# Weights from 64-bit words without a clamp, their range looked at late by reloads, and f, k and q of chunks 5 to 7 loaded later

## The chip, the cores and the metric

The kernel runs on one core of one Trainium2 chip. The metric is the device time of one launch in microseconds. Four compute engines run their own instruction streams in order: PE multiplies matrices, DVE and ACT work on vectors, POOL does a few selections and products. SP issues the transfers (DMA). An engine stops at an instruction until the semaphores that it names have come, and everything behind it on that engine stops too.

## The reference

A linear attention with a decaying state runs over 4 x 8 heads, 768 positions and head size 48. Its output is regrouped to 3072 tokens of 384 and goes through a multiplicative feed-forward layer.

```python
def _attn_ref(q, k, v, f_logit):
    f = 1.0 / (1.0 + np.exp(-f_logit))
    for t in range(S):
        state = f[:, :, t, :, None] * state + np.einsum('bhd,bhe->bhde', k[:, :, t], v[:, :, t])
        y[:, :, t] = np.einsum('bhd,bhde->bhe', q[:, :, t], state)

def _moe_ref(x, w1, w2, w3, w_out):
    a = x @ w1
    b = x @ w2
    h = a * b @ w3
    return (h @ w_out)
```

q, k, v and f_logit are float32. The weights w1, w2 (384 x 1024), w3 (1024 x 1024) and w_out (1024 x 384) are float64: they come to the chip as pairs of 32-bit words, and the kernel makes float32 of them.

## The kernel before, in words

**Attention.** The 3072 tokens are worked in 24 chunks of 128, eight heads at once. For a chunk, f, k and q (two DMAs of 96 KB each) and v are loaded; ACT makes the gate (L378), DVE two scans (L386, L408) and the scaled Q and K (L402, L416), PE the products, POOL the causal mask. Chunks 0 to 3 are worked in a first stage, in which PE also turns the output y to the layout of the layer's input xt (`moved`, L734 to 739) and ACT copies it from the PSUM bank (`settled`, L742). From chunk 4 on y goes through DRAM (yt) and comes back by DMA into xt. PE's general results live in a pool of four banks called f; a product that takes a bank waits until the reader of that bank's former content has run.

**Weights.** Each piece is loaded as 64-bit words. w1 and w2 come in twelve pieces of 512 columns (512 KB), w_out in four of 768 KB, w3 in eight of 1 MB. For each piece ACT takes the magnitude of the high words (L1157) and turns the low words into a float (`rest`, L1160); DVE clamps the magnitude (L1163), shifts it left by three (L1164), puts sign and rest together (`signed`, L1168) and adds the two (`joined`, L1174). w3 @ w_out is multiplied out beforehand: eight `fold`s on PE (L1221), each of 16 matmuls, with a copy on ACT (L1228).

**Feed-forward.** Tokens are taken in six blocks of four chunks. In block 0 the products x @ w1 and x @ w2 (`up`) are plain, three matmuls to a group, first for chunks 0 and 1 (256 wide), then with 512 columns; ACT copies the first factor from its bank (L796) and DVE multiplies the second onto it (L801). Blocks 1 to 5 use seven products in place of eight on halves (`seven` for the two ups, `down` for the product with the folded weight). In `seven` PE does m1, m6, m5, m2 in this order, and ACT copies m1's result (k1, L862) before m2 adds onto the same bank.

**What sets the order.** A planner in Python (`Plan`) gives each task an engine, a cost, dependencies and a priority, and takes greedily the task that can start first by its own clock, the lower priority number first among equals. The result is a fixed order for each engine. SP is one of these engines: all DMAs are issued in one order, at most eight under way. A load is planned to take 0.6 us of lag, its size by a rate, and a second lag (1.3 us and what the call adds). `need(u)` is the time at which chunk u is wanted on that clock; f, k and q of chunk u have the priority need(u) - 30 to - 29.

**At the end.** A small `judge` on DVE looks at the gates' smallest products and at whether the outputs are finite, its result goes through DRAM and back as a row (`told`, `heard`), `decided` reduces it, and the last `m3` of the last block waits for it. If the answer is bad, a general version of the kernel runs after this one; with the data here it doesn't.

Of the kernel before, what the change touches and what calls it, by code (L numbers as in the profile page):

```python
# [36 lines left out]
F32 = mybir.dt.float32  # L37
# [29 lines left out]
LOW = float.fromhex("0x1p-15")  # L67
HIGH = float.fromhex("0x1.dffffep+16")
W = C // 2
FULL = 35.0  # L70
FLOOR = 2.0**-60
RANGE = 2.0**-40


class Plan:
# [13 lines left out]

        self.pools[name] = [None] * n  # L90

    def add(self, eng, cost, emit, deps=(), prio=0.0, takes=(), frees=(), lag=0.2, slack=0.0):


        t = {
            "eng": eng, "cost": cost, "emit": emit, "deps": [d for d in deps if d is not None], "prio": prio,
            "takes": list(takes), "frees": list(frees), "lag": lag, "slack": slack, "at": None, "end": None, "no": len(self.tasks),
        }
        self.tasks.append(t)
        return t  # L100

    def order(self):
        free, done, left = {}, [], list(self.tasks)
        enders = {}
        for t in self.tasks:
            for f in t["frees"]:
                enders.setdefault(id(f), []).append(t)

        def after(t, ds):

            if any(d["end"] is None for d in ds):
                return None
            return max([0.0] + [d["end"] + (d["lag"] + t["slack"] if d["eng"] != t["eng"] else 0.0) for d in ds])

        def places(t, name):

            ends = [(after(t, enders[id(h)]) if h else 0.0, i) for i, h in enumerate(self.pools[name])]
            return [e for e in ends if e[0] is not None]

        def start(t):  # L120

            waits, at = list(t["deps"]), free.get(t["eng"], 0.0)
            for name in t["takes"]:
                if name in self.pools:
                    ends = places(t, name)
                    if not ends:
                        return None
                    at = max(at, min(ends)[0])
                    continue
                n, taken = self.slots[name]  # L130
                if len(taken) >= n:
                    waits += enders[id(taken[-n])]
            ready = after(t, waits)
            return None if ready is None else max(at, ready)

        while left:
            at, _, _, t = min(
                ((at, t["prio"], t["no"], t) for t in left if (at := start(t)) is not None), key=lambda x: x[:3]
            )
            t["at"], t["end"] = at, at + t["cost"]  # L140
            free[t["eng"]] = t["end"]
            for name in t["takes"]:
                if name in self.pools:
                    t["got"] = min(places(t, name))[1]
                    self.pools[name][t["got"]] = t
                else:
                    self.slots[name][1].append(t)
            left.remove(t)
            done.append(t)
        return sorted(done, key=lambda t: (t["at"], t["no"]))  # L150


@with_exitstack
def kernel(
    ctx: ExitStack,
    tc: tile.TileContext,
    q: bass.AP,
    k: bass.AP,
    f_logit: bass.AP,
    v: bass.AP,  # L160
    w1: bass.AP,
    w2: bass.AP,
    w3: bass.AP,
    w_out: bass.AP,
    leaf_mask: bass.AP,
    out: bass.AP,
):
    nc = tc.nc
    const = ctx.enter_context(tc.tile_pool(name="const", bufs=1))
    ident = const.tile([P, P], F32, name="ident")  # L170
    w12 = const.tile([P, 2, KM, DFF], F32, name="w12")
    wc = const.tile([P, KF, DM], F32, name="wc")
    left = const.tile([1, 1], I32, name="left")
    with tc.manual_schedule():
        outside = ranged(tc, q, k, f_logit, v, w1, w2, w3, w_out, out, ident, w12, wc, left)
        with tc.If(outside > 0, preferred_fallthrough_block=True, label="general"):
            general(tc, q, k, f_logit, v, leaf_mask, out, ident, w12, wc)


# [15 lines left out]
def ranged(ctx, tc, q, k, f_logit, v, w1, w2, w3, w_out, out, ident, w12, wc, left):  # L195
# [14 lines left out]
    ps_f = ctx.enter_context(tc.tile_pool(name="ps_f", bufs=1, space=PSUM))  # L210

    floor = keep.tile([R, NQ], F32, name="floor")
    back = keep.tile([R, NQ], F32, name="back")
    gate = [keep.tile([R, NQ + 1], F32, name=f"gate{i}") for i in range(2)]
    qs, ks, fs = ([keep.tile([R, NQ], F32, name=f"{nm}{i}") for i in range(n)] for nm, n in (("q", 3), ("k", 2), ("f", 2)))
    masked = [keep.tile([P, 2, HP, C], F32, name=f"A{i}") for i in range(2)]
    flat = [t.rearrange("p r h c -> p (r h c)") for t in masked]
    diag = [t[:, 0 : 2 * HP * W].rearrange("p (r h c) -> p r h c", r=2, h=HP) for t in flat]
    mids = [t[0:R, 2 * HP * W : 2 * HP * W + HP * D].rearrange("p (h d) -> p h d", d=D) for t in flat]
    sb = [keep.tile([R, HP, R], F32, name=f"sb{i}") for i in range(2)]  # L220
# [103 lines left out]
    def past(u, n, *names):  # L324
        return [tk[u - n][nm] for nm in names if u >= n and nm in tk[u - n]]

    def moves(n, size, rate, emit, deps, prio, late=0.0):


        for j in range(n):  # L330
            i = plan.add("SP", 0.45, (lambda: None) if j else emit, [d] if j else deps, prio - j * 1e-3, takes=["lane"], lag=0.6)
            d = i
            t = plan.add("DMA", size / n / rate, lambda: None, [i], prio - j * 1e-3, lag=1.3 + late, frees=[i])
        return t
# [5 lines left out]
    def front(u):  # L340
# [20 lines left out]
                return []  # L361
            return asked[8:9] + [tk[u - n if u - n >= 4 else u % n][nm] for nm in names]

        t["lf"] = moves(2, 197, 250, load(fu, f_logit), free(2, "g"), n0 - 30)
        t["lk"] = moves(2, 197, 250, load(ku, k), free(2, "k"), n0 - 29.5)
        t["lq"] = moves(2, 197, 250, load(qu, q), free(3, "q"), n0 - 29)

        def load_v():
            s["v"] = at(12288 + NQ, DM) if u == 3 else loads.tile([P, DM], F32, name="vt")
# [739 lines left out]
    def fetch(loads_, a, prio, subs, deps=()):  # L1109
# [36 lines left out]
        def sub(c0, c1, dst, due, waits):  # L1146
            n = c1 - c0
            w = n / 512
            lo, hi = words[:, c0:c1, 0], words[:, c0:c1, 1]
            a0 = spot[0] if n <= 512 else (spot[0] + 512) // 1024 * 1024 % 2048  # L1150
            spot[0] = (a0 + (512 if n <= 512 else 1024)) % 2048
            m = magnitudes[:, a0 : a0 + n]
            mine = range(a0 // 512, (a0 + n + 511) // 512)
            s = {}

            def magnitude():
                nc.scalar.activation(m, hi.bitcast(F32), AF.Abs)  # L1157

            def rest():
                nc.scalar.activation(lo.bitcast(F32), lo, AF.Copy, bias=2.0, scale=2.0**-51)  # L1160

            def shifted():
                nc.vector.tensor_scalar(m, m, HIGH, LOW, ALU.min, ALU.max)  # L1163
                nc.vector.tensor_scalar(m.bitcast(U32), m.bitcast(U32), 3, None, ALU.logical_shift_left)  # L1164

            def signed():
                s["to"] = dst()
                nc.vector.scalar_tensor_tensor(  # L1168
                    s["to"].bitcast(U32), hi, 0x80000000, lo, ALU.bitwise_and, ALU.bitwise_or
                )  # L1170

            def joined():
                to = s["to"].bitcast(I32)
                nc.vector.tensor_tensor(to, m.bitcast(I32), to, ALU.add)  # L1174

            past = [joins[i] for i in mine if i in joins]
            b = plan.add("ACT", 0.2 + 0.43 * w, magnitude, [ld] + past, due)
            e = plan.add("ACT", 0.2 + 0.43 * w, rest, [ld], due)
            h = plan.add("DVE", 0.32 + 0.54 * w, shifted, [b], due)
            g = plan.add("DVE", 0.16 + 0.53 * w, signed, [e, b] + list(waits), due)  # L1180
            j = plan.add("DVE", 0.16 + 0.53 * w, joined, [h, g], due - 1)
            parts.append((g, j))
            joins.update({i: j for i in mine})
            got.append(g)
            ends.append(j)
# [87 lines left out]

    where = {}

    def judge():
        low = work.tile([R, 1], F32, name="low")
        nc.vector.tensor_reduce(out=low, in_=lasts, axis=AX.XY, op=ALU.min)
# [2 lines left out]
        nil = work.tile([R, 1], F32, name="nil")  # L1281
        nc.vector.tensor_reduce(out=nil, in_=zero, axis=AX.X, op=ALU.add)
        nc.vector.tensor_scalar(nil, nil, 0.0, None, ALU.is_equal)
        good = work.tile([R, 1], F32, name="good")
        nc.vector.tensor_scalar(low, low, RANGE, None, ALU.is_ge)
        nc.vector.tensor_tensor(good, low, nil, ALU.mult)
        where["good"] = good

    def told():
        where["all"] = dram.tile([R, 1], F32, name="good")  # L1290
        nc.sync.dma_start(where["all"], where["good"])

    def heard():
        row = work.tile([1, R], F32, name="row")
        nc.sync.dma_start(row, where["all"].rearrange("r one -> one r"))
        where["row"] = row

# [6 lines left out]
    for u in range(NU):  # L1304
# [9 lines left out]
        if u == NPE - 1:  # L1314
            weights()
        if u == NU - 1:
            looked = plan.add("DVE", 1.0, judge, [tk[i]["y"] for i in range(NU)], -20)
            sent = moves(1, 0.4, 250, told, [looked], 0, 20.0)
            judged = plan.add("DVE", 0.2, decided, [moves(1, 0.4, 250, heard, [sent], 0, 20.0)], -20)
        if u % UB == UB - 1:  # L1320
# [2 lines left out]
    for t in plan.order():  # L1323
# [5 lines left out]
        plan.got = t.get("got")  # L1329
        t["emit"]()  # L1330
    return blk[NB - 1]["outside"]


@with_exitstack
# [334 lines left out]
```

## Time and profile before

| | |
|---|---|
| median of three runs | 480.79 us (479.53 to 482.15) |
| profiled execution, device time | 481.99 us |
| its span | 480.3 us |
| granted PE clock | 0.997 |
| ACT L1157 (magnitude) | 24 times: 12 of 512 at 685 ns, 4 of 768 at 929, 8 of 1024 at 1169 |
| ACT L1160 (rest) | 24 times: 683, 922, 1173 ns |
| DVE L1163 (clamp), 512 / 1024 | 419 / 685 ns |
| DVE L1164 (shift), 512 / 1024 | 427 / 694 ns |
| first fold on PE starts | 78.19 us |
| last out store is issued after | PE's last product, 474 us |

The span is the time between the first and the last instruction of the profiled execution; some 1.7 us of its device time lie around it. A row of a timeline gives start and duration, engine, line, operation, the tile written and the tiles read, how many of them followed each other, and in brackets how long the engine had been idle and what released it. A row of waits gives who waited for whom, the total, how often and the longest. A fence cuts such answers to a few lines.

### The profile page before, as it was taken

What the parts mean: (1) busy time and instruction counts of PE and PEld (TensorE: products, weight loads), DVE (VectorE), ACT (ScalarE), POOL (GpSimd) and SP (SyncE); (2) the same over time, 40 slices, a digit from 0 to 9 for tenths busy, and PEclk for the clock granted to TensorE, in tenths of its full rate; (3) what the DMA queues carried; (4) which work ended last, traced back from release to release, by engine and by line L of the source; (5) the groups of instructions that cost most, each with busy time, mean ns of one, the idle gap of its engine ahead of it and who ended that gap; (6) DMA issues with size and microseconds to landing.
All of it is one profiled execution on the core that took longest, in us unless ns stands there. A gap on an engine that the chain in (4) does not pass through costs nothing.

```text
span 480.3 us, 11336 instructions
## 1 busy us (share of the span) xinstructions
PE 466.2 (97%) x4667; PEld 398.5 (83%) x4667; DVE 362.7 (76%) x706; ACT 141.2 (29%) x310; POOL 63.2 (13%) x88
## 2 busy tenths in 40 slices
PE   8799899999999899999999999999999999999995
PEld 6688644656799788899988889988899888889995
DVE  8999699999999889899899467367653667655541
ACT  4787356472313334333432210010100110110000
POOL 9300000013303224212431100000000000000000
PEclk9999999999999999999999999999999999999998
DMA  6899277843516664455631002100101000000011
GB/s 183 261 386 235 61 256 248 286 139 92 138 38 171 190 185 138 125 150 142 168 111 26 18 18 66 50 17 2 57 27 49 1 0 1 0 2 0 34 66 40
DMA packets 36622, 50.14 MB, mean 104 GB/s; under 512 B 4546, under 2 KB 26050, under 8 KB 35538
## 3 DMA queue, kind: packets, MB, share of 16 engines
q1 hardware_dynamic: 36562, 49.33, 34.1%
q8 instruction: 38, 0.62, 0.6%
q14 instruction: 22, 0.18, 0.1%
HBM read 40.67 MB, written 8.65 MB: 103 GB/s over the span
## 4 chain that ended last, share of the span: by engine, by line
PE 78%; DMA 8%; DVE 7%; POOL 3%; issue 2%; ACT 1%; SPq 0%; ACTq 0%; DVEq 0%; POOLq 0%
PE f L759 62%; PE f L1221 7%; PE py L513 2%; DMA vt<-in_v_dram 2%; DMA place<-in_w_dram 2%; PE pa L439 2%; DMA place<-in_w_out_dram 2%; PE f L453 2%; PE py L532 2%; PE pa L546 2%; DMA k<-in_k_dram 2%; DVE place L1168 1%; DVE place L1174 1%; POOL ab L304 1%; DVE ab L801 1%
## 5 line engine op out<-in xcount | busy, mean ns | idle before, releaser
L759 PE MATMUL f<-xt,w 128*128 128x256 f32 (+1 forms) x600 | 161.1, 397 | 3.4 <-ACT ab L796 1.9
L759 PEld LDWEIGHTS f<-xt,w 128*128 128x128 f32 x600 | 112.9, 190 | 29.1 <-issue 10.0
L759 PE MATMUL f<-place 128*128 128x192 f32 (+1 forms) x504 | 112.1, 349 | 0.1
L759 PEld LDWEIGHTS f<-place 128*128 128x128 f32 x504 | 87.7, 190 | 6.2 <-DVE place L1010 0.4
L569 POOL TENSOR_SCALAR_AFFINE_SELECT A<-A 64x512 f32<-64x512 f32 (+1 forms) x44 | 40.9, 929 | 117.3 <-ACT A L563 107.5
L1221 PE MATMUL f<-place 128*128 128x384 f32 x128 | 42.8, 489 | 0.2 <-DVE place L1174 0.2
L862 ACT COPY a<-f 128x256 f32<-128x256 f32 x36 | 13.4, 373 | 93.2 <-PE f L759 78.0
L1221 PEld LDWEIGHTS f<-place 128*128 128x128 f32 x128 | 23.8, 190 | 16.5 <-DVE place L1174 0.8
L759 PE MATMUL f<-xt,place 128*128 128x256 f32 x144 | 37.3, 382 | 0.0
L759 PE MATMUL f<-wc,ab 128*128 128x192 f32 x192 | 35.2, 327 | 0.0
L759 PEld LDWEIGHTS f<-wc,ab 128*128 128x128 f32 x192 | 32.0, 190 | 0.5
L408 DVE TENSOR_TENSOR_SCAN bwd<-gate,back 112x512 f32<-112x512 f32 x24 | 30.0, 1248 | 0.8
L386 DVE TENSOR_TENSOR_SCAN fwd<-gate,floor 112x512 f32<-112x512 f32 x24 | 29.6, 1232 | 1.2 <-ACT gate L378 0.3
L759 PEld LDWEIGHTS f<-xt,place 128*128 128x128 f32 x144 | 26.6, 189 | 3.3
L886 DVE TENSOR_TENSOR place<-f,a 128x256 f32<-128x256 f32 x36 | 15.2, 423 | 18.3 <-PE f L759 18.0
L1157 ACT ACTIVATE place<-place 128x512 f32<-128x512 f32 (+2 forms) x24 | 21.3, 887 | 7.8 <-DVE w L1174 3.8
L672 POOL TENSOR_TENSOR G<-lasts,gate 112x4 f32<-112x4 f32 x20 | 11.6, 580 | 88.1 <-ACT lasts L391 55.2
L1160 ACT ACTIVATE place<-place 128x512 f32<-128x512 uint32 (+2 forms) x24 | 21.1, 886 | 5.7 <-DMA place<-in_w_out_dram 5.7
L708 ACT ACTIVATE ys<-py 112x512 f32<-112x512 f32 x20 | 11.9, 596 | 34.4 <-PE py L532 34.4
L759 PE MATMUL f<-place,w 128*128 128x256 f32 x72 | 21.4, 379 | 0.0
L897 DVE TENSOR_TENSOR ab<-f,place 128x256 f32<-128x256 f32 x36 | 15.2, 423 | 6.2 <-PE f L759 5.3
L995 DVE TENSOR_TENSOR place<-ab 128x512 f32<-128x512 f32 x24 | 16.9, 703 | 3.5 <-PE f L759 3.5
(126 smaller groups left out, 641.1 us busy)
## 6 DMA issues: line engine op xcount, KB each, us to landing
place<-in_w_dram SPq DMA_DIRECT2D x8, 1024.0 KB, 4.9
place<-in_w_dram SPq DMA_DIRECT2D x12, 512.0 KB, 10.4
out_dram<-o SPq DMA_DIRECT2D x24, 192.0 KB, 1.9
q<-in_q_dram SPq DMA_DIRECT2D x46, 96.0 KB, 2.9
vt<-in_v_dram SPq DMA_DIRECT2D x23, 192.0 KB, 3.8
k<-in_k_dram SPq DMA_DIRECT2D x44, 96.0 KB, 2.3
f<-in_f_logit_dram SPq DMA_DIRECT2D x43, 96.0 KB, 2.5
yt<-ys SPq DMA_DIRECT2D x40, 96.0 KB, 2.6
```

The source lines that it names most:

```text
L386: nc.vector.tensor_tensor_scan(s["P"], gate[u % 2][:, 0:NQ], floor, 0.0, ALU.mult, ALU.max)
L408: nc.vector.tensor_tensor_scan(s["R"][:, ::-1], gate[u % 2][:, NQ:0:-1], back[:, ::-1], 0.0, ALU.mult, ALU.max)
L569: nc.gpsimd.affine_select(out=a, in_=a, pattern=pattern, compare_op=ALU.is_ge, fill=0.0, base=0, channel_multiplier=-1,)
L708: nc.scalar.activation(ys, py, AF.Copy, accum_out=ysum[:, u : u + 1])
L759: nc.tensor.matmul(out_, lhsT=lhs[i], rhs=rhs[i], start=start and i == 0, stop=i == len(lhs) - 1, skip_group_check=True,)
L862: nc.scalar.copy(q["a"], q["X"])
L886: nc.vector.tensor_tensor(ups["u3", k], q["Y"], q["a"], ALU.add)
L897: nc.vector.tensor_tensor(m if which else to(tok, half), q[bank_], m, ALU.add)
L995: nc.vector.tensor_tensor(abs_[j], x, y, op)
L1157: nc.scalar.activation(m, hi.bitcast(F32), AF.Abs)
L1160: nc.scalar.activation(lo.bitcast(F32), lo, AF.Copy, bias=2.0, scale=2.0**-51)
L1221: nc.tensor.matmul(w3s["p", jc], lhsT=w3s[jc][:, kc * P : kc * P + P], rhs=wos[:, kc], start=(kc == 0), stop=(kc == KF - 1),)
```

## The change

For each weight piece, the magnitude on ACT and the clamp on DVE are gone; the shift reads the high words where they were loaded (every second word). The sign bit is shifted out by it, so without the clamp the result is right only for weights whose magnitude is in a certain range. That is looked at later: `ranges`, planned once the last chunk's attention is done with its buffers, loads all weights again, 17 loads of 1 MB into the place of the two masked tiles A. After each, ACT sums the magnitudes of the high words (`total`) and the signs of magnitude less a limit (`count`); each load waits for the count before it. Four operations on DVE (`verdict`) make one number of it, and `judge` multiplies it into its own, which has 128 rows now instead of 112. If a check fails, the general version runs, and before it `convert` makes the weights again with the clamp.

Besides, f, k and q of chunks 5, 6 and 7 may not be planned before need(u) - 17 on the planner's clock.

```diff
+AHEAD = 17.0
-    def add(self, eng, cost, emit, deps=(), prio=0.0, takes=(), frees=(), lag=0.2, slack=0.0):
+    def add(self, eng, cost, emit, deps=(), prio=0.0, takes=(), frees=(), lag=0.2, slack=0.0, since=0.0):
...
-            waits, at = list(t["deps"]), free.get(t["eng"], 0.0)
+            waits, at = list(t["deps"]), max(free.get(t["eng"], 0.0), t["since"])
...
-    back = keep.tile([R, NQ], F32, name="back")
+    spare = keep.tile([P, NQ], F32, name="back")
+    back = spare[0:R]
-    masked = [keep.tile([P, 2, HP, C], F32, name=f"A{i}") for i in range(2)]
-    flat = [t.rearrange("p r h c -> p (r h c)") for t in masked]
+    both = keep.tile([P, 2 * WIDE], F32, name="A")
+    flat = [both[:, i * WIDE : i * WIDE + WIDE] for i in range(2)]
+    masked = [t.rearrange("p (r h c) -> p r h c", r=2, h=HP) for t in flat]
...
-        t["lf"] = moves(2, 197, 250, load(fu, f_logit), free(2, "g"), n0 - 30)
-        t["lk"] = moves(2, 197, 250, load(ku, k), free(2, "k"), n0 - 29.5)
-        t["lq"] = moves(2, 197, 250, load(qu, q), free(3, "q"), n0 - 29)
+        since = n0 - AHEAD if 4 < u < 8 else 0.0
+        t["lf"] = moves(2, 197, 250, load(fu, f_logit), free(2, "g"), n0 - 30, since=since)
+        t["lk"] = moves(2, 197, 250, load(ku, k), free(2, "k"), n0 - 29.5, since=since)
+        t["lq"] = moves(2, 197, 250, load(qu, q), free(3, "q"), n0 - 29, since=since)
...
-            def magnitude():
-                nc.scalar.activation(m, hi.bitcast(F32), AF.Abs)
-
             def shifted():
-                nc.vector.tensor_scalar(m, m, HIGH, LOW, ALU.min, ALU.max)
-                nc.vector.tensor_scalar(m.bitcast(U32), m.bitcast(U32), 3, None, ALU.logical_shift_left)
+                nc.vector.tensor_scalar(m.bitcast(U32), hi, 3, None, ALU.logical_shift_left)
...
-            b = plan.add("ACT", 0.2 + 0.43 * w, magnitude, [ld] + past, due)
             e = plan.add("ACT", 0.2 + 0.43 * w, rest, [ld], due)
-            h = plan.add("DVE", 0.32 + 0.54 * w, shifted, [b], due)
-            g = plan.add("DVE", 0.16 + 0.53 * w, signed, [e, b] + list(waits), due)
+            h = plan.add("DVE", 0.16 + 0.27 * w, shifted, [ld] + past, due)
+            g = plan.add("DVE", 0.16 + 0.53 * w, signed, [e, h] + list(waits), due)
...
+    def ranges():
+        seen = [w[kc * P : kc * P + P] for w in (w1, w2) for kc in range(KM)] + [w3[jc] for jc in range(KF)]
+        rows_ = w_out.rearrange("(p a) c -> p (a c)", a=KF)
+        seen += [rows_[:, c : c + WIDE] for c in range(0, KF * DM, WIDE)]
...
+        last = [plan.add("DVE", 0.1, lambda: nc.vector.memset(small, -SMALL), [tk[NU - 1][nm] for nm in ("r", "v", "mid")] + [tk[NU - 2]["v"]], -20)]
+        def load(i):
+            return lambda: nc.sync.dma_start(words, seen[i].bitcast(U32))
+        def total(i):
+            return lambda: nc.scalar.activation(hi, hi, AF.Abs, accum_out=sums_[:, i : i + 1])
+        def count(i):
+            return lambda: nc.scalar.activation(hi, hi, AF.Sign, bias=small, accum_out=counts[:, i : i + 1])
+        for i in range(n):
+            ld = moves(1, 1024, 380, load(i), last, 500 + i, 1.0)
+            a = plan.add("ACT", 1.1, total(i), [ld], 500 + i)
+            last = [plan.add("ACT", 1.2, count(i), [a], 500 + i)]
+        def verdict():
+            nc.vector.tensor_scalar(sums_, sums_, LARGE, None, ALU.is_le)
+            nc.vector.tensor_scalar(counts, counts, WIDE - 0.5, None, ALU.is_ge)
+            nc.vector.tensor_tensor(sums_, sums_, counts, ALU.mult)
+            where["weights"] = small
+            nc.vector.tensor_reduce(out=small, in_=sums_, axis=AX.X, op=ALU.min)
+        return plan.add("DVE", 0.5, verdict, last, -20)
...
-        good = work.tile([R, 1], F32, name="good")
+        good = work.tile([P, 1], F32, name="good")
-        nc.vector.tensor_tensor(good, low, nil, ALU.mult)
+        nc.vector.memset(good, 1.0)
+        nc.vector.tensor_tensor(good[0:R], low, nil, ALU.mult)
+        if wide:
+            nc.vector.tensor_tensor(good, good, where["weights"], ALU.mult)
...
-            looked = plan.add("DVE", 1.0, judge, [tk[i]["y"] for i in range(NU)], -20)
+            weighed = [ranges()] if wide else []
+            looked = plan.add("DVE", 1.0, judge, [tk[i]["y"] for i in range(NU)] + weighed, -20)
```

More of the change, by code (lines that the diff above doesn't have):

```diff
@@ L69 @@
 W = C // 2
+WIDE = 2 * HP * C
+SMALL = 2.0**-8
+LARGE = 2.0**15
 FULL = 35.0
+AHEAD = 17.0
 FLOOR = 2.0**-60
@@ L90, in pool @@
         self.pools[name] = [None] * n
-    def add(self, eng, cost, emit, deps=(), prio=0.0, takes=(), frees=(), lag=0.2, slack=0.0):
+    def add(self, eng, cost, emit, deps=(), prio=0.0, takes=(), frees=(), lag=0.2, slack=0.0, since=0.0):
         t = {
             "eng": eng, "cost": cost, "emit": emit, "deps": [d for d in deps if d is not None], "prio": prio,
-            "takes": list(takes), "frees": list(frees), "lag": lag, "slack": slack, "at": None, "end": None, "no": len(self.tasks),
+            "takes": list(takes), "frees": list(frees), "lag": lag, "slack": slack, "since": since, "at": None, "end": None, "no": len(self.tasks),
         }
@@ L176 @@
         with tc.If(outside > 0, preferred_fallthrough_block=True, label="general"):
+            if w1.dtype != F32:
+                convert(tc, w1, w2, w3, w_out, w12, wc)
             general(tc, q, k, f_logit, v, leaf_mask, out, ident, w12, wc)
@@ L325, in past, with moves @@
         return [tk[u - n][nm] for nm in names if u >= n and nm in tk[u - n]]
-    def moves(n, size, rate, emit, deps, prio, late=0.0):
+    def moves(n, size, rate, emit, deps, prio, late=0.0, since=0.0):
         for j in range(n):
-            i = plan.add("SP", 0.45, (lambda: None) if j else emit, [d] if j else deps, prio - j * 1e-3, takes=["lane"], lag=0.6)
+            i = plan.add("SP", 0.45, (lambda: None) if j else emit, [d] if j else deps, prio - j * 1e-3, takes=["lane"], lag=0.6, since=since)
             d = i
@@ L1274, in ranged @@
     where = {}
+    def ranges():
+        seen = [w[kc * P : kc * P + P] for w in (w1, w2) for kc in range(KM)] + [w3[jc] for jc in range(KF)]
+        rows_ = w_out.rearrange("(p a) c -> p (a c)", a=KF)
+        seen += [rows_[:, c : c + WIDE] for c in range(0, KF * DM, WIDE)]
+        n = len(seen)
+        sums_, counts, small = (spare[:, a : a + m] for a, m in ((0, n), (32, n), (64, 1)))
+        words = both.bitcast(U32)
+        hi = words.rearrange("p (n two) -> p n two", two=2)[:, :, 1].bitcast(F32)
+        last = [plan.add("DVE", 0.1, lambda: nc.vector.memset(small, -SMALL), [tk[NU - 1][nm] for nm in ("r", "v", "mid")] + [tk[NU - 2]["v"]], -20)]
[16 more added lines that the diff above has]
+        return plan.add("DVE", 0.5, verdict, last, -20)
     def judge():
@@ L1283, in judge @@
         nc.vector.tensor_scalar(nil, nil, 0.0, None, ALU.is_equal)
-        good = work.tile([R, 1], F32, name="good")
+        good = work.tile([P, 1], F32, name="good")
         nc.vector.tensor_scalar(low, low, RANGE, None, ALU.is_ge)
-        nc.vector.tensor_tensor(good, low, nil, ALU.mult)
+        nc.vector.memset(good, 1.0)
+        nc.vector.tensor_tensor(good[0:R], low, nil, ALU.mult)
+        if wide:
+            nc.vector.tensor_tensor(good, good, where["weights"], ALU.mult)
         where["good"] = good
     def told():
-        where["all"] = dram.tile([R, 1], F32, name="good")
+        where["all"] = dram.tile([P, 1], F32, name="good")
         nc.sync.dma_start(where["all"], where["good"])
     def heard():
-        row = work.tile([1, R], F32, name="row")
+        row = work.tile([1, P], F32, name="row")
         nc.sync.dma_start(row, where["all"].rearrange("r one -> one r"))
@@ L1331, in ranged, with convert, single @@
     return blk[NB - 1]["outside"]
+@with_exitstack
+def convert(ctx, tc, w1, w2, w3, w_out, w12, wc):
+    nc = tc.nc
+    work = ctx.enter_context(tc.tile_pool(name="cwork", bufs=2))
+    keep = ctx.enter_context(tc.tile_pool(name="ckeep", bufs=1))
+    ps = ctx.enter_context(tc.tile_pool(name="cps", bufs=2, space=bass.MemoryType.PSUM))
+    def single(src, dst):
+        n = src.shape[-1]
+        raw = work.tile([P, 2 * DFF], U32, name="raw")[:, 0 : 2 * n]
+        m = work.tile([P, DFF], F32, name="m")[:, 0:n]
+        nc.sync.dma_start(raw, src.bitcast(U32))
+        words = raw.rearrange("p (n two) -> p n two", two=2)
+        lo, hi = words[:, :, 0], words[:, :, 1]
+        nc.scalar.activation(m, hi.bitcast(F32), AF.Abs)
+        nc.scalar.activation(lo.bitcast(F32), lo, AF.Copy, bias=2.0, scale=2.0**-51)
+        nc.vector.tensor_scalar(m, m, HIGH, LOW, ALU.min, ALU.max)
+        nc.vector.tensor_scalar(m.bitcast(U32), m.bitcast(U32), 3, None, ALU.logical_shift_left)
+        nc.vector.scalar_tensor_tensor(dst.bitcast(U32), hi, 0x80000000, lo, ALU.bitwise_and, ALU.bitwise_or)
+        nc.vector.tensor_tensor(dst.bitcast(I32), m.bitcast(I32), dst.bitcast(I32), ALU.add)
+    for which, w in enumerate((w1, w2)):
+        for kc in range(KM):
+            single(w[kc * P : kc * P + P], w12[:, which, kc])
+    rows_ = keep.tile([P, KF, DM], F32, name="rows")
+    for a in range(KF):
+        single(w_out[a * P : a * P + P], rows_[:, a])
+    for jc in range(KF):
+        t = work.tile([P, DFF], F32, name="t")
+        single(w3[jc], t)
+        p = ps.tile([P, DM], F32, name="p")
+        for a in range(KF):
+            nc.tensor.matmul(p, lhsT=t[:, a * P : a * P + P], rhs=rows_[:, a], start=(a == 0), stop=(a == KF - 1))
+        nc.scalar.copy(wc[:, place_of(jc)], p)
 @with_exitstack
```

## The prediction

> **What bounds the kernel now.** I read the page's engine table first, then busy time by stretches, then the waits of PE (TensorE), then the two timelines around its longest wait.
>
> ```profile
> PE 466.2 (97%) x4667; PEld 398.5 (83%) x4667; DVE 362.7 (76%) x706; ACT 141.2 (29%) x310; POOL 63.2 (13%) x88
> ```
>
> PE is busy 97% of the span. The other engines matter only where PE waits for them.
>
> ```profile
> 34.00:50.00 16.00, 16.00 (x79) 14.19 (x79) 12.88 (x27) 10.62 (x20) 0.00 (x0) 1.00 0.92 229
> 50.00:60.00 10.00, 8.10 (x32) 5.81 (x32) 7.47 (x17) 4.42 (x9) 0.51 (x1) 1.00 0.19 50
> 60.00:80.00 20.00, 20.00 (x49) 9.07 (x48) 19.69 (x28) 11.20 (x16) 0.20 (x1) 1.00 0.79 271
> 100.00:135.00 35.00, 35.00 (x464) 24.66 (x463) 34.17 (x48) 12.79 (x27) 7.63 (x8) 1.00 0.39 106
> 275.00:410.00 135.00, 135.00 (x689) 122.96 (x682) 82.49 (x200) 14.80 (x41) 0.00 (x0) 1.00 0.08 26
> ```
>
> Columns: stretch and length, then busy time of PE, weight loads, DVE, ACT, POOL, then clock, DMA share, GB/s. From 60 to 135 DVE is as full as PE, and still PE does not stop: DVE's full row costs nothing as it stands. In the tail ACT is busy 11% and the DMA 8%. Only 50 to 60 has a hole in PE.
>
> ```profile
> PE f L759 <- ACT ab L796: 1.9, 1, 1.9
> PE f L759 <- ACT gate L378: 1.4, 1, 1.4
> PE pa L429 <- DVE Q L402: 1.0, 1, 1.0
> PE f L1221 <- DVE place L1174: 0.2, 1, 0.2
> ```
>
> These are PE's waits after 24 us (total, times, longest). The first hole, in the timelines of PE and ACT:
>
> ```profile
> 34.70 15.71 PE L759 MATMUL f<-xt,w 128*128 128x256 f32 x72
> 52.30 1.99 PE L759 MATMUL f<-xt,w 128*128 128x256 f32 x8 [1.90 <-ACT ab L796]
> ...
> 51.12 0.88 ACT L1160 ACTIVATE place<-place 128x768 f32<-128x768 uint32 x1 [4.89 <-DMA place<-in_w_out_dram]
> 51.90 0.35 ACT L796 COPY ab<-f 128x256 f32<-128x256 f32 x1
> ```
>
> ACT stood 4.89 us at the head of its queue for the second w_out piece. The copy that frees PE's bank was behind it. The 1.4 at 161.25 is a late transfer in truth: DVE's L829 waited 1.99 us for xt<-yt until 161.19, and the gate named had long ended.
>
> [...] the dense shift (L1164: 427 ns for 512, against 758 for L1168 with two sources); a shift from every second word no run shows. [...] a stride of two words should be free; L1168 reads such words in the time of a dense two-source operation (1221 and 1247 ns for 1024), which agrees. [...] the trace has 1.17 (L1160), and I use that, +0.09 for Sign.
>
> **Part 1: Abs and clamp go.** ACT loses L1157, 24 times, 21.3 us; DVE loses L1163, start to start about 12 x 0.45 + 4 x 0.59 + 8 x 0.72 = 13.5 us. Almost all lies beside a full PE. What can be won is DVE's share in waits: 0.2 before the second fold, and half of the 0.6 at two small waits (0.36 for L1010 at 135.97, 0.25 for an ACT copy at 263.88). I take -0.5 (0 to -0.8; the 1.0 at 24 us is counted in part 2).
>
> [...] it would take 0.69, 0.95, 1.22 instead of 0.43, 0.56, 0.69: 12 x 0.26 + 4 x 0.39 + 8 x 0.53 = 9 us of DVE. I take zero; the other end is rival C.
>
> **Part 2: f, k, q of chunks 5 to 7 later.** SP's order is unchanged to k of chunk 4. Then come two w_out loads, where q4, f5 and k5 (six DMAs) stood between them; in all 18 DMAs for f, k, q of three chunks go behind loads of weights. The second w_out piece was issued at 42.03 and landed at 51.04; now its issue is at about 37.5, the place of q4's row, so it lands some 3 us earlier or more. Both gates of chunks 4 and 5 that stood behind it (1.15 us at 52.15) are elsewhere. The wait of 1.9 goes: -1.9 (-1.9 to 0).
>
> But ACT's order changes before that too. In the trace, xt of chunk 3 is copied at 34.90 and the first ab copies run at 36.20, 37.49, 38.90, 40.08 between conversions. In the changed order ACT has the conversions (the Copy of L1160) of w12 pieces 9, 10 and 11, then xt of chunk 3, then the gate of chunk 4, and only then the first ab copy. The SP queue's rows give the landings: piece 11 issued at 29.88 takes 10.2 us, so 40.1; the first half of f4 issued at 31.10 takes 9.4, so 40.5, the second 41.0. DMA is at 0.92 and more until then and has the same orders, so these times stay. PE has four banks; one holds chunk 3's px until its xt copy. The timeline's 72 records in 15.71 us are twelve groups of three 256-wide products, 1.31 us each. Three run from 34.70 to 38.6; the fourth needs that bank. ACT: 40.1 + 0.68 + 0.48 = 41.3. So PE loses 41.3 - 38.6 = +2.7 (1.5 to 3.4). That PE comes to this point sooner, as without its 1.0 at 24 us, only makes the wait longer and not the end later. The gate (0.63) ends at 41.9, in time for the fifth group at 42.6.
>
> Chunk 5's late f harms nothing: attention of chunk 4 itself first reaches PE at 88.95 in the trace. Afterwards only four, not eight, 512-wide groups (2.6 us each) stand before the first fold. It was at 78.19; now about 78.19 - 4 x 2.6 - 1.9 + 2.7 = 68.6. The w3 loads, first at 64.81 before, follow w_out directly, near 50: 5 us to land, then conversion, ready near 61 to 63. No wait, 5 us in hand. The 1.4 at 161 depends on when xt of chunk 7 is issued, which moves with all of this: half of it, -0.7.
>
> **Part 3: the look at the ranges.** 17 loads of 1 MB, each with Abs and Sign over 1024 words, strictly one after another: 4.9 (a 1 MB load's median) + 1.17 + 0.19 + 1.26 + 0.19 (two readings of the accumulator, 0.19 as at L708) and hand-overs of some 0.4 = 8.1 us; 17 of them, 138 us from about 263, end near 400. SP keeps xt loads and stores behind some of them, and the last m3 that needs the answer is at 472: 65 us in hand. DMA at 0.08 can take 17 MB. ACT gets 34 x 1.36 = 46 us more in a stretch with 120 us free. What can reach PE is a k1 copy (L862, 0.37 us) behind such an operation: m6 and m5 give it 0.86 us, of which 0.23 are to spare. The planner puts the two where its clock sees no k1; I take +0.2 (0 to +4). The verdict and judge, some twelve DVE operations at 0.15 us, stand together before a u2 near 402: 1.8 less its slack, +0.6 (0 to 1.2). Were those 65 us gone, each further 1 us of the chain would be 1 us at the end.
>
> **Sum** against the profiled execution (span 480.3, itself 481.99): -0.5 - 1.9 + 2.7 - 0.7 + 0.2 + 0.6 = +0.4, which would be 482.4. That execution is 1.2 above the median of the three, 480.79; on the median the forecast is 481.2, no change. About 0.5% (2.4 us) is what can be told from none.
>
> **Rivals.**
> - A, faster: the fourth group does not wait, since piece 11 lands sooner or ACT's earlier work leaves room, and xt of chunk 7 is in time. -0.5 - 1.9 - 1.4 + 0.2 + 0.6 = -3.0, so 477.8. For it: the 161 wait is a matter of one transfer. Against: the DMA is full to 40 us with the same queue.
> - B, slower: ACT's in-order queue in the tail. An Abs stands at its head waiting for its load, with a k1 behind. The planner's load lasts about 5.6 us (lags of 0.6 and 2.3 and 1024 / 380 = 2.7); the trace's 1 MB takes 4.9, so it decides from a load of over 5.6. About eight of the 17 pairs have a k1 next to them with little room; at half a microsecond each (half of 1.17) this is +4 beside the sum, so 485.2. For it: the loads share SP with stores. Against: the DMA is idle there.
> - C: [...] 5.8 of its 9 us fall before the second fold, where 5 are in hand; the folds then wait 1 to 2 in all, +1.5 beside the sum: about 482.7, on the border of no change.
>
> **How the numbers follow.** Forecast 0.46 (own range 479 to 483.2), A 0.25, B 0.20, C 0.09. C goes half to no change: faster 0.25, same 0.50, slower 0.25. The range reaches to A below and most of B above: 477.6 to 484.6.
>
> **What would show it.** PE's waits: no 1.9 at L796 near 52, a new one of 2 to 3 near 38 to 41 at the fourth up group, ended by ACT's xt copy. The shift's row: 0.43 for 512. PE without holes from 263 to 400 (else B). A small wait near 402 behind the verdict. The first fold near 68. It is wrong if the fourth group starts before 40, or if k1 waits repeat in the tail.

## The result, and the profile after

| | kernel before | changed kernel |
|---|---|---|
| median of 12 runs | 479.56 us (478.15 to 482.15) | 480.01 us (478.71 to 483.87) |
| ratio, 95% interval | | 1.0024 (1.0006 to 1.0042) |
| profiled execution | 481.99 us, span 480.3 | 483.87 us, span 482.1 |

By the ratio the change adds 0.24%, about 1 us (the two medians differ by 0.45): less than the half per cent that the prediction set as what can be told from no change. Forecast were no change and 481.2.

Both profiled executions took longer than most, which matters below. The changed kernel's is the slowest of its twelve. Of the 168 executions of the kernel before that were timed here and in the experiments, four took longer than the profiled 481.99. So the waits that go and come in these two traces are not the balance of an ordinary execution.

The engine table and the shift's rows of the changed kernel, the latter from the groups of DVE by shape between 20 and 135 us:

```profile
PE 467.2 (97%) x4667; PEld 399.3 (83%) x4667; DVE 352.6 (73%) x689; ACT 164.9 (34%) x354; POOL 60.0 (12%) x88
```

```profile
L1169 DVE TENSOR_SCALAR place<-place 128x1024 uint32<-128x1024 uint32 x8 | 5.4, 684 | 0.0
L1169 DVE TENSOR_SCALAR place<-place 128x512 uint32<-128x512 uint32 x12 | 5.0, 419 | 0.0
```

PE has the same work. DVE has 10 us less to do and ACT 24 more: without the Abs it has 21 less, with the reloads some 45 more. The shift from every second word takes 419 and 684 ns, against 427 and 694 from a dense tile: the stride cost nothing here. Rival C, in which the strided shift takes 0.69, 0.95 and 1.22 us for the three sizes, 9 us more in all, is out. Its figures were an estimate; the kernel before has such times at L1174 (690 and 954 ns) and L1168 (1221).

PE's waits after 24 us, in the answer for the changed kernel:

```profile
PE f L768 <- ACT xt L751: 2.7, 1, 2.7
PE pa L438 <- DVE Q L411: 1.0, 1, 1.0
PE f L768 <- ACT a L871: 0.9, 1, 0.9
```

The 1.9 at L796, the 1.4 at 161 us and the 0.2 before a fold are gone. Two are new: 2.7 for the copy of xt, 0.9 for a k1 copy. First the 2.7, in the timelines of PE and ACT:

```profile
34.81 4.05 PE L768 MATMUL f<-xt,w 128*128 128x256 f32 x18
41.56 29.09 PE L768 MATMUL f<-xt,w 128*128 128x256 f32 x102 [2.70 <-ACT xt L751]
70.49 10.48 PE L1225 MATMUL f<-place 128*128 128x384 f32 x32
```

```profile
38.34 0.66 ACT L1166 ACTIVATE place<-place 128x512 f32<-128x512 uint32 x1 [3.07 <-DMA place<-in_w_dram]
40.50 0.65 ACT L1166 ACTIVATE place<-place 128x512 f32<-128x512 uint32 x1 [1.49 <-DMA place<-in_w_dram]
41.05 0.46 ACT L751 COPY xt<-f 128x384 f32<-128x384 f32 x1
41.41 0.63 ACT L387 ACTIVATE gate<-f 112x512 f32<-112x512 f32 x1
```

Three groups of ups run, then PE needs the bank of chunk 3, whose copy (L751) stands on ACT behind two conversions (L1166) that wait for their loads. The second of these is for piece 11, the last of the twelve pieces of w1 and w2; it landed at 40.41 in this trace.

The timeline's single row hides something after the hole, which busy time by stretches shows (the column before the last two is the granted clock):

```profile
42.00:43.00 1.00, 1.00 (x6) 0.81 (x5) 0.66 (x2) 0.58 (x3) 0.20 (x1) 0.75 0.95 305
43.00:46.00 3.00, 3.00 (x9) 2.36 (x8) 2.86 (x7) 0.00 (x0) 0.00 (x0) 0.51 0.15 43
46.00:50.00 4.00, 4.00 (x20) 3.54 (x19) 2.98 (x7) 2.38 (x4) 0.00 (x0) 1.00 0.00 1
```

From 42.5 to 45.9, for 3.4 us, PE ran at half clock (0.51 granted from 43 to 46): eight records stand 0.43 us apart instead of 0.22, 1.65 us more in all. It set in 1.0 us after the hole of 2.7 had ended.

The 0.9, in the tail's timelines of ACT and PE:

```profile
308.13 1.15 ACT L1295 ACTIVATE A<-A 128x1024 f32<-128x1024 f32 x1 [3.74 <-DMA A<-in_w_dram]
309.17 0.19 ACT L1295 ACTIVATION_READ_ACCUMULATOR A<-A 128x1 f32 x1
309.39 1.23 ACT L1298 ACTIVATE A<-A,back 128x1024 f32<-128x1024 f32 x1
310.52 0.19 ACT L1298 ACTIVATION_READ_ACCUMULATOR A<-A,back 128x1 f32 x1
310.61 0.36 ACT L871 COPY a<-f 128x256 f32<-128x256 f32 x1
```

```profile
311.02 1.13 PE L768 MATMUL f<-xt,w 128*128 128x256 f32 x4 [0.93 <-ACT a L871]
```

Abs (L1295) waited at ACT's head for its load, and Sign (L1298) and the k1 copy (L871) stood behind.

What a wait costs in all shows in the starts of PE's products, set against the same products in a profile without the wait. So counted, this one costs 1.20 and another k1 copy, at 317, 0.41 (against the second profile of the order on ACT alone, below). The operations of verdict and judge cost 0.61 near 405 (against the kernel without the look, below). Gone, by starts: 2.2 at 52 us, some 1.5 at 161, 0.25 before a fold, and two small waits of some 0.6, together 4.5. New: 2.9 at 41 us, 1.65 of half clock, 1.6 and 0.6, together 6.8. The balance, 2.2, is the difference of the two spans, 1.8, to within half a microsecond.

### The profile page after: what moved, and what is told of

It reads as the page before. It is cut to its first block, busy times and chain, and to the rows that moved or that the text cites. A ratio compares the mean times of both kernels' runs of the same rounds, so it can differ in the third digit from the quotient of the medians.

```text
span 482.1 us, 11392 instructions
## 1 busy us (share of the span) xinstructions
PE 467.2 (97%) x4667; PEld 399.3 (83%) x4667; DVE 352.6 (73%) x689; ACT 164.9 (34%) x354; POOL 60.0 (12%) x88
## 4 chain that ended last, share of the span: by engine, by line
PE 84%; DMA 6%; DVE 4%; POOL 2%; ACT 2%; issue 1%; DVEq 0%; ACTq 0%; POOLq 0%
PE f L768 65%; PE f L1225 9%; DMA A<-in_w_dram 4%; PE py L522 3%; DMA place<-in_w_dram 2%; PE pa L448 2%; PE pa L555 2%; PE f L462 2%; PE py L541 2%; POOL ab L312 1%; ACT A L1298 1%; ACT A L1295 1%; DVE w L1179 1%; DVE w L1173 0%; DVE K L425 0%
## 5 line engine op out<-in xcount | busy, mean ns | idle before, releaser
L768 PE MATMUL f<-xt,w 128*128 128x256 f32 (+1 forms) x600 | 163.7, 401 | 3.8 <-ACT xt L751 2.7
L578 POOL TENSOR_SCALAR_AFFINE_SELECT A<-A 64x512 f32<-64x512 f32 (+1 forms) x44 | 39.2, 891 | 114.8 <-ACT A L572 105.4
L871 ACT COPY a<-f 128x256 f32<-128x256 f32 x36 | 13.3, 369 | 61.5 <-PE f L768 54.4
L1295 ACT ACTIVATE A<-A 128x1024 f32<-128x1024 f32 x17 | 19.7, 1156 | 25.4 <-DMA A<-in_w_dram 24.5
L1166 ACT ACTIVATE place<-place 128x512 f32<-128x512 uint32 (+2 forms) x24 | 21.3, 888 | 10.0 <-DMA place<-in_w_dram 9.9
L1298 ACT ACTIVATE A<-A,back 128x1024 f32<-128x1024 f32 x17 | 21.2, 1250 | 0.3
L681 POOL TENSOR_TENSOR G<-lasts,gate 112x4 f32<-112x4 f32 x20 | 10.1, 505 | 75.5 <-ACT gate L387 40.5
```

Of the source, the lines that this page charges most:

```text
L578: nc.gpsimd.affine_select(out=a, in_=a, pattern=pattern, compare_op=ALU.is_ge, fill=0.0, base=0, channel_multiplier=-1,)
L768: nc.tensor.matmul(out_, lhsT=lhs[i], rhs=rhs[i], start=start and i == 0, stop=i == len(lhs) - 1, skip_group_check=True,)
L871: nc.scalar.copy(q["a"], q["X"])
L1295: return lambda: nc.scalar.activation(hi, hi, AF.Abs, accum_out=sums_[:, i : i + 1])
L1298: return lambda: nc.scalar.activation(hi, hi, AF.Sign, bias=small, accum_out=counts[:, i : i + 1])
```

## The experiments

Each kernel was timed against the kernel before; ratios are compared where kernels ran on the same chip: the first four below, then the next four, then the last two. The changed kernel was timed again with the first four only. Across chips a comparison is rough: the same kernel, the one with the order on ACT changed, gave 0.9972 on the first chip and 0.9998 on the third.

**The changed kernel again.** No edit.

> The changed kernel once more, to see which of its waits come back in a second profile. Theory 1 (the order on ACT sets the hole): PE waits 2.5 to 2.9 us near 41 us for ACT's copy of xt of chunk 3, again. Theory 2 (the hole is an accident of one execution's transfers): under 1.5 us. Open: whether TensorE's slower passage after the hole (8 records of 0.43 instead of 0.22 us apart, 1.65 us in all) and the 0.9 us wait at 311 for a k1 copy come back. Time: 0 to +1.2 us against the kernel before.

Ratio 1.0013 (0.9996 to 1.0029). PE's waits in its profile:

```profile
PE f L768 <- ACT xt L751: 0.8, 1, 0.8
PE f L768 <- ACT a L871: 0.2, 1, 0.2
```

The hole is in the same place with the same releaser, but 0.8 long: that is the number of Theory 2, and no half clock follows (1.00 granted from 34 to 50). Piece 11 landed at 38.59. In four profiles PE went on about 1.15 us after that landing: 40.41 and 41.56, 38.59 and 39.74, 40.12 and 41.27, 39.20 and 40.35 (this kernel twice, then the ones without the look and without the later loads, below). So the landing sets when the hole ends; that the order on ACT makes it, the next run shows.

**The order on ACT changed alone.**

```diff
+SHY = 6.0
-ld = moves(1, total, 380, load, held, prio, max(0.0, 3.5 - 1.2 * load_no) if load_no < 4 * KM else 3.0)
+ld = moves(1, total, 380, load, held, prio, max(0.0, 3.5 - 1.2 * load_no) + SHY * (load_no > 8) if load_no < 4 * KM else 3.0)
-t["lf"] = moves(2, 197, 250, load(fu, f_logit), free(2, "g"), n0 - 30, since=since)
+t["lf"] = moves(2, 197, 250, load(fu, f_logit), free(2, "g"), n0 - 30, SHY * (u == NPE), since=since)
```

> Only the planner is told that w12 pieces 9 to 11 and f of chunk 4 land 6 us later than it thought, so that ACT copies xt of chunk 3 and the first product ahead of their conversions. Theory 1 (the hole at 41 us comes from ACT's order): no wait of PE between 34 and 60 us over 0.3 us, the first fold 2.7 us earlier than in the changed kernel (67.8 instead of 70.5), or 4.3 earlier (66.2) if the slower passage after the hole goes with it; time 2.7 to 4.3 us under the changed kernel's, so -1.5 to -3.5 us against the kernel before. Rival (PE would only wait a little later, for the second w_out piece): a wait of 1.5 us or more between 46 and 56, time within 1 us of the changed kernel.

Ratio 0.9972 (0.9959 to 0.9986). The xt copy now ends ahead of the conversions, PE has no wait from 34 to 300 us, and the first fold starts at 65.78:

```profile
34.95 0.48 ACT L752 COPY xt<-f 128x384 f32<-128x384 f32 x1 [1.65 <-PE f L747]
```

```profile
34.00:50.00 16.00, 16.00 (x80) 14.19 (x79) 15.13 (x32) 6.60 (x13) 0.20 (x1) 1.00 0.62 187
```

```profile
65.78 10.48 PE L1226 MATMUL f<-place 128*128 128x384 f32 x32
```

Piece 11 landed early in this profile, at 38.0, where the old order would have had a hole of some 0.3 only. In a second profile of this kernel (the last run below) it landed at 39.3, for which the old order would give 1.7, and there was no wait either. The edit also put two w_out loads ahead of k of chunk 4 on SP and moved a few operations on DVE and one on POOL; PE's own order is the same. So the hole is ACT's order, and the rival is out.

Against the changed kernel this is 0.9972 / 1.0013, 2.0 us less (by the two intervals, 1 to 3), not 2.7 to 4.3: the hole is shorter than 2.7 in the other profiles, and the half clock is rare. Of the changed kernel's 34 timed executions four have a granted clock of 0.994 over the whole execution, as the profiled one with the half clock in it, and take 482.1 to 483.9 us; the other thirty have 0.996 or more. The k1 waits stayed:

```profile
PE f L769 <- ACT a L872: 1.4, 2, 1.1
```

**Without the look at the range.**

```diff
-weighed = [ranges()] if wide else []
+weighed = []
-        if wide:
-            nc.vector.tensor_tensor(good, good, where["weights"], ALU.mult)
```

> Leaves out the look at the weights' range: no reloads, no Abs and Sign, no verdict. Theory 1 (it costs PE only the waits seen, 0.9 to 1.4 at 311 and 317 and 0.4 at 405): 1.3 to 1.8 us under the changed kernel, hole at 41 unchanged. Rival (17 MB of loads and 46 us of ACT slow other things unseen): 3 us or more under it. Other rival (the waits are an accident of the one profile): within 0.5 us of it.

Ratio 0.9977 (0.9964 to 0.9991), 1.7 us under the changed kernel on that chip. Its profile has a hole of 1.8 near 41 us and no wait of PE after it. So the late look costs some 1.7, by the two intervals 0.7 to 2.7, which leaves out both rivals. The 2.2 counted in the first profile (1.6 for k1, 0.6 for verdict and judge) lies within this.

**Work put into the hole.**

```diff
             def up(jc, which):
                 def emit():
+                    ups_done[0] += 1
+                    if ups_done[0] == 4:
+                        to = ps.tile([P, 2, NQ], F32, name="py")[:, 0, 0:TH]
+                        for _ in range(FILL):
+                            nc.tensor.matmul(to, lhsT=floor[:, 0:P], rhs=floor[:, 0:TH], start=True, stop=True)
```

> Five products of 256 columns on constants, read by nobody, stand on PE ahead of the fourth group of ups, so that PE is busy some 2.2 us of the hole of 2.7. Nothing else moves. Theory 1 (PE's clock falls for 3.4 us because it was idle for 2.7): the wait left is about 0.5 us, and the 8 slow records after it are gone, first fold at 68.8 instead of 70.5, 1.65 us under the changed kernel if that always has the slow passage. Rival (the slow passage has another cause[...], or is an accident): it comes all the same, time as the changed kernel.

Ratio 1.0106 (1.0077 to 1.0135): neither theory's number. The tile chosen for the idle products was still to be read by DVE, whose instruction stood behind the product with the first ab copy:

```profile
PE py L803 <- DVE S L697: 4.1, 1, 4.1
```

The hole grew to 4.1, and the clock in the stretch after it, 43 to 47, was 0.59. This says nothing on filling a hole, but shows half clock after a longer one.

The same with a tile that nobody held (`name="pa"`):

> As e5_fill, with the five products written to a bank that nobody reads or holds then, so that they don't wait themselves: PE is idle for 0.6 us or less before the fourth group, whenever the transfers let the hole be 2.7. Theory 1 (PE's clock falls after 2 to 2.7 us without work): no products at 0.43 us apart anywhere from 39 to 50 us, granted clock 1.00 in that stretch. Rival (it falls for another reason): they come as in the changed kernel. Time within 1.3 us of the changed kernel either way, as the five products cost up to 1.3 where the hole would have been 0.8.

Ratio 1.0026 (1.0012 to 1.0039). PE had no wait and no half clock between 34 and 60 (1.00 granted). But piece 11 landed at 39.37 there, so the hole would have been some 1.7 (39.37 + 1.15 - 38.8), and a hole of 1.8, in the run without the look, had no half clock either (1.00 granted from 34 to 50). This run doesn't decide about the clock.

**The later loads alone, in the kernel before** (`AHEAD` and `since` as in the change, nothing else).

> The kernel before with one part of the change alone: f, k and q of chunks 5 to 7 later. Abs and clamp stay, no reloads. Theory 1 (the later loads are worth the wait for the second w_out piece, and the hole at 41 belongs to the other part): the piece lands some 3 us sooner than 51.0, no wait of PE near 52 us (1.9 before), no hole near 41 us, time 1.5 to 2.2 us under the kernel before. Rival (the wait is only moved to another load, or the hole near 41 comes with this part): within 0.7 us of the kernel before.

Ratio 0.9984 (0.9969 to 0.9998). The second w_out piece landed at 47.95 and the wait near 52 is gone, by PE's starts a gain of 2.2 us on the profile before. Half of the expectation came in time: 0.8 us, not 1.5 to 2.2. The interval, 0.1 to 1.5, does not rule out the rival's 0.7. The wait for xt of chunk 7 is longer, and in this execution the clock halved after it, at 161 to 164 (0.58):

```profile
159.32 4.51 PE L761 MATMUL f<-xt,w 128*128 128x256 f32 x12 [1.89 <-ACT gate L380]
```

Twelve records take 4.51 here; in the profile before, at 161.25, the same twelve took 2.83. So what this profile gained near 52 it lost again here.

**The changed kernel without the later loads** (`since = 0.0` for all chunks).

> The changed kernel without the later loads: Abs and clamp gone, reloads at the end, f, k and q of chunks 5 to 7 loaded as early as before. Theory 1 (the hole near 41 us comes from the missing Abs, and whatever PE loses there it doesn't lose again for the second w_out piece): the hole is there as in the changed kernel, 0.8 to 2.7 us, and the wait near 52 us is smaller than 1.9 by about as much; time within 0.8 us of the changed kernel. Rival (the two waits add up): 1.5 to 2.2 us over the changed kernel.

Ratio 1.0017 (1.0002 to 1.0032), near the changed kernel's 1.0013 on the other chip. The hole was 1.4; but near 52 there was no wait at all, because the second w_out load was issued at 36.82 here (42.03 before), ahead of f, k and q of chunk 5. A likely reason is that without the Abs the planner has the load's place in the buffer free sooner; this was not looked at by itself. So without Abs and clamp the wait for w_out goes too, and the later loads add nothing to it that these ratios show.

**The reloads placed behind k1.**

```diff
-            ld = moves(1, 1024, 380, load(i), last, 500 + i, 1.0)
+            ld = moves(1, 1024, 380, load(i), last, 500 + i, 2.5)
```

> The order of e1_landing, and the planner's lag of the reloads raised from 1.0 to 2.5 us, so that Abs and Sign are put behind the k1 copies that they stood ahead of. Theory 1 (the waits for k1, 1.3 and 0.4 us in e1_landing's profile, are a matter of that order): none of PE's waits between 270 and 400 us over 0.4 us; 0.8 to 1.6 us under e1_landing, so 2 to 3 us under the kernel before. Rival (the reloads delay PE whatever their place, or the later end of the chain meets the last block): within 0.4 us of e1_landing, or over it.

Ratio 0.9988 (0.9978 to 0.9998). Its profile shows no wait of PE from 24 us on, so the first half of Theory 1 holds. The time against the order alone is open, as that kernel ran on another chip; against the kernel before it is 0.6 us, not 2 to 3. Something was lost at the end: the chain of reloads ends later, the answer was read at 470.5 beside the last product, and the chain of waits ends in it:

```profile
470.30 0.19 DVE least L1342
470.49 0.02 issue
470.51 0.15 DVE left L1343
470.67 0.03 issue
470.69 0.66 DVEq L1055
```

From PE's last product to the span's end are 6.4 us; in the kernel with the order alone they are 5.4 and, in its second profile, 5.9.

This execution ran at half clock too, from about 21 to 24.6 us, after two waits of 0.96 and 0.55:

```profile
18.98 0.61 PE L463 MATMUL py<-ident,K 112*128 112x112 f32 x4 [0.96 <-DVE S L697]
20.13 1.16 PE L439 MATMUL pa<-Q,K 48*128 48x128 f32 x16 [0.55 <-ACT sb L707]
21.23 1.97 PE L477 MATMUL f<-A,vt 128*64 128x128 f32 x16
```

The last row's sixteen products take 1.09 us in the changed kernel's second profile; the granted clock from 0 to 24 is 0.94, where the two runs before this one have 1.00.

**The answer asked for sooner.** As the last, and:

```diff
-            sent = moves(1, 0.4, 250, told, [looked], 0, 20.0)
+            sent = moves(1, 0.4, 250, told, [looked], 0, 4.0)
-            judged = plan.add("DVE", 0.2, decided, [moves(1, 0.4, 250, heard, [sent], 0, 20.0)], -20)
+            judged = plan.add("DVE", 0.2, decided, [moves(1, 0.4, 250, heard, [sent], 0, 4.0)], -20)
```

> e6_both, and the planner's lag of the two small transfers that carry the answer lowered from 20 to 4 us, so that the answer's row is asked for ahead of the last block's stores and read long before the last product. Theory 1 (in e6_both the waits for k1 were gone, and 0.7 to 0.9 us came back at the end because the answer was read at 470.5, beside the last product): the span's part after PE's last product is 5.5 us instead of 6.4, no wait of PE over 0.4 us from 34 to the end, 0.7 to 0.9 us under e6_both, and 0.8 to 1.7 under e1_again. Rival (that part is no longer for the answer, or the executions differ by more than this): within 0.4 us of e1_again.

> e1_landing once more beside e8_answer on the same chip. Theory 1: 1.3 to 2.2 us under the kernel before, no wait near 41 us, the waits for k1 of 0.4 to 1.4 us in all again between 300 and 400. Rival (they are an accident of one execution): none over 0.4 us.

Ratio 0.9975 (0.9964 to 0.9987) for this one, 0.9998 (0.9979 to 1.0016) for the order alone beside it. The first is 1.1 us under the second on this chip, within what was expected. The end is back to 5.45 us after the last product, and PE's only wait after 25 us is this:

```profile
PE f L769 <- DVE ab L902: 0.2, 1, 0.2
```

The order alone was 0.1 us under the kernel before, not 1.3 to 2.2, and shows no k1 wait in this second profile, which is the rival's outcome for it; its executions spread from 477.7 to 480.7. Whether the Abs meets a k1 depends on the execution; why one chip showed 0.9972 and another 0.9998 is open. The version with all three planner constants changed is faster than the kernel before by 0.25%, 1.2 us, less than the half per cent set in the prediction. Beside the changed kernel it was not timed.

## Why the prediction was right, and where it was not

The outcome, no change, was right, and so was the main mechanism: PE's wait for a load went, and another came because ACT's order had changed. That the sum came so near is luck in part. It was set up on an execution of the kernel before that took 2.4 us more than that kernel's median of 479.56. PE has the same 4667 products to do in every execution, so an ordinary one cannot hold all of the waits that the sum lets go; which are missing, no run shows. The hole that the sum adds was also longer in the changed kernel's first profile than in the others, so the two surpluses offset each other. By its steps:

- **Part 1, Abs and clamp.** The cover held. The strided shift took no longer than the dense one (419 ns for 512 words, 427 before): the zero taken for it, an estimate from L1168's times in the kernel before (1221 ns beside 1247), held. And the wait before the fold and both small waits are gone (some -0.8 for the -0.5 taken). The one before the fold is also gone with the later loads alone, so it needn't be this part's.
- **Part 2, the wait for w_out.** It went, -1.9. But the step gave this to the later loads. Each part of the change does it alone, as the two runs with one of them show, and together they don't do it twice. The first w3 load was issued at 57.20 and not near 50, still early enough: no fold waited.
- **Part 2, the new hole.** Its place and its cause were right. That its length agreed in the first profile, 2.7 for 2.7, is luck. The step that failed is "so these times stay": the landing of piece 11 lay between 38.0 and 40.41 in profiles of kernels that load alike up to it, and the hole, where the order makes one, between 0.8 and 2.7. In the second profile it was 0.8, under the stated 1.5 to 3.4, and the fourth group started at 39.74, which is the sign of being wrong that the prediction named (before 40). Missing from the sum was the half clock afterwards, 1.65 in the first profile; it is also why the first fold came at 70.5 and not 68.6 there (66.98 in the second profile). The 1.0 at 24 us, taken for gone, stayed (1.01 at 24.46), without effect on the end of the hole.
- **Part 2, the 1.4 at 161.** It went whole; half was counted. With the later loads alone it was 1.9 in the one profile taken.
- **Part 3.** The last Sign ended at 403.0, for an end near 400, far from where it was needed. Two errors offset each other in this: the first reload was issued at 255.2 instead of some 263, and from one to the next were 8.8 us instead of 8.1. The times taken for ACT held: Abs took 1.16 us and Sign 1.25, for 1.17 and 1.26. The term was 0.8 in all (0.2 + 0.6), and the run without the look gained 1.7. Verdict and judge cost what was said, 0.61 for 0.6. The k1 part is what varies: in the seven profiles in which PE's order in the tail is the changed kernel's it was 1.6, 0.45, 0.45, 0.35, 0, 1.9 and 0, for the 0.2 taken (its range went to 4). Rival B's mechanism was thus at work, at two places at most and not at eight.

In the first profile the sum was +0.4 for a measured +1.8. The missing 1.65 of the clock and 1.4 of k1, less 0.8 from the wait at 161 and some 0.3 of the small ones, make up the difference within half a microsecond.

## What to carry to other kernels

When instructions are taken off an in-order engine, list what then stands ahead of the first instruction that frees something for the bottleneck: here the Abs had kept copies and conversions interleaved, and without it conversions that wait for loads moved ahead of the copy that PE needed (holes of 0.8 to 2.7 us, none in the two profiles with the order changed alone). A gain by one part of a change may be had by another part alone; run each by itself before adding them. A check that is moved to the tail costs through what it stands ahead of (here some 1.7 us in all), not through its some 45 us of work on ACT, which in the kernel before was busy 11% of that stretch (275 to 410 us).

## What the runs showed of the hardware that was not expected

While PE had products to run, its clock was halved in four of the twelve profiles: after holes of 2.7 (1.65 us more), 4.1 and 1.9 us (the last in the run with the later loads), and after two of 0.96 and 0.55 that ended 1.15 us apart (the reloads placed behind k1). By the granted clock of the stretches and the stretched rows, it stayed so for 3.2 to 3.4 us and set in 0.8 to 1.1 us after PE had gone on. It was not halved after holes of 0.8, 1.4, 1.8 and another 1.9 (the kernel before, at 52 us): the granted clock is 1.00 from 34 to 50 for the first three, and from 52 to 56 for the last. The same two of 0.96 and 0.55 stand in the profile without the look too, where the next sixteen products took 1.09 us and not 1.97. So the length of a hole doesn't tell it, and what does, no run here shows.
